# One clamp instead of two when float64 weights are converted, load targets in the result slots, and a compact RMS norm for batches 0 and 1

## The chip, the cores and the metric

The kernel runs on one core of one Trainium2 chip. The metric is the time of one execution in device microseconds. Three runs of the kernel before took 1404.11 to 1405.84 us, with a median of 1405.21 us.

## What is computed

Three stages follow each other. For 8 batches, 8 heads, 576 tokens and 64 features, linear attention (no softmax) with an RMS norm; then a feed-forward stage whose hidden layer is the maximum of three products; then one with a squared ReLU:

```python
kv = einsum('bhsd,bhse->bhde', k, v)
out = einsum('bhsd,bhde->bhse', q, kv)
out = out / sqrt(mean(out * out, axis=-1) + 1e-6) * g_norm      # per head
x = out as [8*576, 512]
h = maximum(maximum(x @ w1, x @ w2), x @ w3)                     # 512 -> 768
x = h @ w_out                                                    # 768 -> 512
r = maximum(x @ w_in, 0)                                         # 512 -> 2048
out = (s * (r * r) + b) @ w_out2                                 # 2048 -> 512
```

q, k, v and g_norm arrive as float32. The weight matrices arrive as float64 and are read by the kernel as 16-bit words, four to an element. Products are made in float32r as three matmuls of high and low parts (`mm3`: high times high, high weight times low activation, low weight times high activation), so each weight and each activation is split once into a high part (ScalarE, a rounding copy) and a low part (VectorE or GpSimd, a subtraction; both go through `hi_part` and `lo_part`, L263 and L266).

## The kernel before

Tokens are taken as 9 tiles of 512: tile j holds the first 512 tokens of batch j, the ninth the last 64 tokens of all batches. A tile is feature-major, 128 partitions (two heads, h and h + 4 of one **chunk** p, p = 0 to 3) by 512 tokens.

**Order of the work.** Nearly all work up to the last batch is written as jobs: `job(position, engine, cost, function, ..., r, w, a)` names what is read, written and allocated. `arrange` (L71) takes jobs in order of position as priorities: on each engine it starts the ready job with the lowest place in that order, as soon as the engine is free by the planner's own costs, and the list so made is issued as it stands. So each engine (PE, ACT, DVE, POOL) and the load queue SP runs its instructions in that fixed order, and waits where the real times differ from the planner's. A tag has a ring of buffers (`SIZE`; one where nothing is said), and a job that allocates waits for the last use of the buffer that it takes. Positions count in weight tiles; batch 0's start stands at Z = -12 and later, batch j's first layer at 22 j.

**Attention.** `load_kv`, `load_rem` and `load_q` (L301 to L333) bring k, v and q per chunk; `kv_mm` (L318) makes k^T v; `q_turn` (L337, VectorE) transposes q; `o_mm` (L350, L356) multiplies two chunks (half u) into one PSUM tile with tag "o" of two banks (one buffer), in quarters of 64x64; `o_out` (L360, ScalarE) copies it to SBUF.

**Norm, per chunk** (`plan_norm`): square (L366, ScalarE); `ms_mm` (L385, TensorE) multiplies by a 128x128 matrix that holds 1/64 in two blocks, so that each of the 64 rows of a head holds its mean square: for batches 0 and 1 (`bb < PLAIN`) one float32 matmul, which shows in the trace as two records; `rsqrt` (L394, L396, L399, ScalarE: logarithm, exponential, square) and `newton` (L404, L406, L409, VectorE): one Newton step and the multiplication by g. Then `x_hi` and `x_lo` split the chunk. Batches 2 to 7 split the square, too (`sq_hi`, `sq_lo`).

**First layer.** 18 weight tiles w0 to w17 (128 columns of w1, w2 or w3 in turn, all 512 rows: 128 partitions x 512 elements), each used by 12 matmuls (L155 to L157) per token tile (`plan_g1`); every three of them end in a copy and two maxima (L439, L441) and a split of h. For batch 0, w0 to w3 are used chunk by chunk as chunks are finished; from w4 on a tile takes all four chunks. **Second layer:** 6 tiles o0 to o5 (`plan_g2`).

**Conversion of a float64 tile** (`plan_conv`, 24 tiles before and beside batch 0, 32 later ones p0 to p31 that are stored again as float32): `conv_load` (L213, SP) brings 512 KB, moved by one 16-bit word; `conv_c` (L221 ScalarE or, for every third w and o tile and all p tiles, L223 VectorE) clears the sign of the upper 16 bits into a tile of its own; `conv_t` (L237, L239, ScalarE) are two ReLUs that clamp the exponent from above and from below; `conv_r` (L228, VectorE) scales and clamps the mantissa; `conv_s` (L232, VectorE) sets the sign; `conv_sum` (L243, VectorE) joins both; `conv_hi` and `conv_lo` split the result into the pair slot w0 to w17 or o0 to o5. The 512 KB land in one of three staging tiles: `craw`, and two of the slots of o0 to o5, which are not yet used.

```python
def conv_t(key, n):
    t = st["tr", key][:, 0]
    if n == 0:
        act(out=t.bitcast(F32), in_=st.pop(("gc", key)), func=AF.Relu, scale=-1.0, bias=lim[:, 0:1])
    else:
        act(out=t, in_=t.bitcast(F32), func=AF.Relu, scale=-float(2 ** 19), bias=lim[:, 1:2])
...
    sets = [("craw", "ctr", "cgc"), tuple(WOS[3:]), tuple(WOS[:3])]
```

After the batches the second feed-forward stage runs in products of quarters with fewer multiplications (L761, L839); the change does not touch it.

## Time and profile before

| | |
|---|---|
| median of three runs | 1405.21 us |
| the profiled execution | 1407.22 us |
| its span, first to last instruction | 1405.40 us |
| mean granted TensorE clock | 0.999 of 2.4 GHz |
| TensorE busy | 1370.8 us (98%), 6960 matmuls |
| VectorE busy | 908.3 us (65%) |
| ScalarE busy | 760.0 us (54%) |
| GpSimd busy | 244.4 us (17%) |
| DMA | 202.5 MB, 144 GB/s over the span |

The span is one execution on the hardware profiler. Shares are means over stages with different limits, so the stretches of the span are to be read one by one. A matmul record is longer than the matmul's share of the engine, since matmuls overlap: in an unbroken stream the starts tell the pace. "Clock" is the clock that TensorE was granted, as a part of 2.4 GHz.

### The profile page before, as it was taken

The numbers are of one execution on the slowest core, as the hardware profiler recorded it, in microseconds if no ns is written. First come the engines' busy times: TensorE is split into PE (matmuls) and PEld (weight loads), VectorE is DVE, ScalarE is ACT, GpSimd is POOL, SyncE is SP. The second block draws the span as 40 slices with busy tenths as digits, with TensorE's granted clock in tenths as the row PEclk, the third lists the DMA queues.
The fourth block names the chain that finished last, engine by engine and source line by source line (L and its number), as shares of the span: only waits on it lengthen the run. The fifth ranks groups of instructions, "written<-read, shape, count | busy, mean of one in ns | idle before, by whom it ended". The sixth has DMA issues, their size and how long they took to land. (4 is left out here: it accounts for less than half of the span.)

```text
span 1405.4 us, 19416 instructions
## 1 busy us (share of the span) xinstructions
PE 1370.8 (98%) x6960; PEld 1118.7 (80%) x6960; DVE 908.3 (65%) x1460; ACT 760.0 (54%) x1345; POOL 244.4 (17%) x173
## 2 busy tenths in 40 slices
PE   5999999999999999999999999999999999999997
PEld 3768888888888888888788789877888888888887
DVE  5995736363646452444747757467877978888884
ACT  6884435253434342333556456556775656566565
POOL 0001313132323122211000000000003314141412
PEclk9999999999999999999999999999999999999999
DMA  9876263625453310030354635544684454544441
GB/s 244 236 212 161 68 175 92 168 76 156 98 155 79 105 46 30 1 120 0 124 209 172 236 144 195 173 163 160 207 301 151 147 198 150 180 148 148 155 143 38
DMA packets 229169, 202.52 MB, mean 144 GB/s; under 512 B 126032, under 2 KB 183376, under 8 KB 226896
## 3 DMA queue, kind: packets, MB, share of 16 engines
q1 hardware_dynamic: 228912, 201.02, 46.1%
q8 instruction: 54, 0.88, 0.3%
q14 instruction: 43, 0.35, 0.1%
q10 hardware_dynamic: 160, 0.26, 0.0%
HBM read 126.79 MB, written 74.45 MB: 143 GB/s over the span
## 5 line engine op out<-in xcount | busy, mean ns | idle before, releaser
L155 PE MATMUL g<-xh,w_w 128*128 128x512 f32 x648 | 257.6, 398 | 0.7 <-ACT h L439 0.6
L156 PE MATMUL g<-xl,w_w 128*128 128x512 f32 x648 | 253.1, 391 | 1.5 <-DVE xl L266 1.5
L157 PE MATMUL g<-xh,w_w 128*128 128x512 f32 x648 | 253.3, 391 | 0.1
L151 ACT ACTIVATE zx<-z 128x512 fp32r<-128x512 f32 (+1 forms) x280 | 161.3, 587 | 123.1 <-PE zs_a L839 35.2
L761 PE MATMUL ps_a<-x_q,w_q 128*128 128x512 f32 (+1 forms) x960 | 210.5, 371 | 5.2 <-DVE cs L669 4.1
L839 PE MATMUL zs_a<-zx,w_q 128*128 128x512 f32 (+1 forms) x960 | 203.8, 369 | 0.5 <-POOL zx L152 0.3
L761 PEld LDWEIGHTS ps_a<-x_q,w_q 128*128 128x128 f32 x960 | 167.1, 188 | 40.0 <-DVE cs L669 7.2
L152 DVE TENSOR_TENSOR zx<-z,zx 128x512 fp32r<-128x512 f32 (+1 forms) x234 | 172.5, 755 | 34.8 <-ACT zx L151 34.5
L839 PEld LDWEIGHTS zs_a<-zx,w_q 128*128 128x128 f32 x960 | 167.9, 188 | 32.0 <-POOL zx L152 0.7
L152 POOL TENSOR_TENSOR zx<-z,zx 128x512 fp32r<-128x512 f32 (+1 forms) x46 | 64.3, 1398 | 594.1 <-DMA gd<-cs 382.6
L441 DVE TENSOR_TENSOR h<-g,h 128x512 f32<-128x512 f32 x108 | 74.6, 691 | 136.0 <-PE g L157 130.5
L155 PEld LDWEIGHTS g<-xh,w_w 128*128 128x128 f32 x648 | 121.8, 188 | 29.1 <-ACT xh L263 1.5
L156 PEld LDWEIGHTS g<-xl,w_w 128*128 128x128 f32 x648 | 122.0, 188 | 28.3 <-DVE xl L266 2.8
L157 PEld LDWEIGHTS g<-xh,w_w 128*128 128x128 f32 x648 | 121.8, 188 | 27.1 <-DVE w_w L266 0.7
L266 POOL TENSOR_TENSOR h<-h,h 128x512 fp32r<-128x512 f32 x40 | 60.1, 1504 | 458.4 <-ACT h L263 458.4
L761 PE MATMUL ps_b<-x_q,w_q 128*128 128x512 f32 (+1 forms) x480 | 106.4, 369 | 1.6 <-ACT cs L772 1.1
L839 PE MATMUL zs_b<-zx,w_q 128*128 128x512 f32 (+1 forms) x480 | 103.9, 371 | 2.0 <-DVE zx L152 2.0
L263 ACT ACTIVATE h<-h 128x512 fp32r<-128x512 f32 x54 | 34.0, 630 | 126.1 <-DVE h L441 125.5
L839 PEld LDWEIGHTS zs_b<-zx,w_q 128*128 128x128 f32 x480 | 83.9, 188 | 19.0 <-DVE zx L152 3.3
L761 PEld LDWEIGHTS ps_b<-x_q,w_q 128*128 128x128 f32 x480 | 83.9, 188 | 18.1 <-ACT cs L772 1.8
L155 PE MATMUL g<-h,w_o 128*128 128x512 f32 x216 | 84.6, 391 | 0.0
L157 PE MATMUL g<-h,w_o 128*128 128x512 f32 x216 | 84.0, 389 | 0.0
(149 smaller groups left out, 2016.7 us busy)
## 6 DMA issues: line engine op xcount, KB each, us to landing
z<-gd SPq DMA_DIRECT2D x64, 512.0 KB
gd<-cs SPq DMA_DIRECT2D x96, 256.0 KB
z<-gd SPq DMA_DIRECT2D x48, 256.0 KB
x1d<-x SPq DMA_DIRECT2D x36, 256.0 KB
k<-in_k_dram SPq DMA_DIRECT2D x32, 256.0 KB
...
```

Of the source, the lines that this page charges most:

```text
L151: act(out=hi, in_=src, func=AF.Copy)
L152: eng.tensor_tensor(out=lo, in0=src, in1=hi.bitcast(F32), op=ALU.subtract)
L155: nc.tensor.matmul(ps, lhsT=w[:, 0, sl], rhs=xh, start=first, stop=False)
L156: nc.tensor.matmul(ps, lhsT=w[:, 0, sl], rhs=xl, start=False, stop=False)
L157: nc.tensor.matmul(ps, lhsT=w[:, 1, sl], rhs=xh, start=False, stop=last)
L263: act(out=out, in_=src, func=AF.Copy)
L266: eng.tensor_tensor(out=out, in0=src, in1=hi.bitcast(F32), op=ALU.subtract)
L441: nc.vector.tensor_tensor(out=st["h", m], in0=ps, in1=st["h", m], op=ALU.max)
L761: nc.tensor.matmul(ps, lhsT=w[:, a, c], rhs=x[:, b_], start=new and k == 0 and e == 0, stop=k == HK - 1 and e == 2, skip_group_check=True)
L839: nc.tensor.matmul(ps, lhsT=w[:, a, c], rhs=x[:, b_, :n], start=new and k_ == 0 and e == 0, stop=k_ == 3 and e == 2, skip_group_check=True)
```

## The change

Conversion: the absolute value is written into the fourth 16-bit word of each element of the raw tile itself (`mag16`), on ScalarE for all w and o tiles and on VectorE for the p tiles; a single ReLU with a scale of 2^19 and a bias of -896 x 2^23 gives the exponent; for odd w and o tiles (`QACT`) the mantissa is made on ScalarE as its complement, and the join becomes an exclusive or and an or in one operation. Every w and o tile is loaded into the slot that its own result will take; the intermediate tile `tr` of the w tiles rotates over `craw`, `ctr` and the slots of o5 and o4. Positions of the first loads and conversions move (w0 to w3: loads from -10.65, -9.65, ... to -8.65, -8.35, ...; conversions one later), and those of batch 0's first matmuls by 0.5.

Norm of batches 0 and 1: the four squares have four buffers (`SQ`); `msc_mm` multiplies a square by a 128x32 matrix whose first two columns hold 1/64 for one head each, into rows 32p to 32p+31 of one PSUM tile; `rsqrt_c` makes logarithm, exponential, square and two Newton operations once for two chunks (batch 0, 64 partitions) or four (batch 1, 128 partitions); `bc_mm` multiplies 32 rows by `spread`, which holds ones where a head's row is to go to its 64 output rows, for two chunks into one PSUM tile with tag "o"; `normed` (VectorE) multiplies o by g and by that. `spread` is made of an identity (`make_identity`, two GpSimd operations) by eight small VectorE operations with the memsets of `means`.

```diff
-    nc.vector.memset(lim[:, 0:1], float(1151 * 16))
-    nc.vector.memset(lim[:, 1:2], float(255 * 2 ** 23))
+    nc.vector.memset(lim[:, 0:1], -float(896 * 2 ** 23))
+    nc.vector.memset(lim[:, 1:2], float(2 ** 19 - 1))
...
+    means = at_.tile([P, 32], F32, name="means")
+    nc.vector.memset(means, 0.0)
+    for h in range(2):
+        nc.vector.memset(means[h * D:(h + 1) * D, h:h + 1], 1.0 / D)
+    ident = at_.tile([P, P], F32, name="ident")
+    make_identity(nc, ident)
+    pick = at_.tile([P, 16], F32, name="pick")[:, :2]
+    spread = at_.tile([P, 2, D], F32, name="spread")
+    nc.vector.tensor_tensor(out=pick, in0=ident[:, 0:2], in1=ident[:, 32:34], op=ALU.add)
+    for p in range(2, NP):
+        nc.vector.tensor_tensor(out=pick, in0=pick, in1=ident[:, 32 * p:32 * p + 2], op=ALU.add)
+    for h in range(2):
+        nc.vector.tensor_copy(out=spread[:, h], in_=pick[:, h:h + 1].to_broadcast([P, D]))
...
-    def conv_c(key, gc, eng):
-        st["gc", key] = gc()
+    def mag16(key):
+        return st["raw", key].rearrange("p (n f) -> p n f", f=4)[:, :, 3]
+    def conv_c(key, eng):
...
-            act(out=st["gc", key].bitcast(BF16), in_=top16(key).bitcast(BF16), func=AF.Abs)
+            act(out=mag16(key).bitcast(BF16), in_=top16(key).bitcast(BF16), func=AF.Abs)
...
-            ts(out=st["gc", key], in0=top16(key), scalar1=0x7FFF, scalar2=None, op0=ALU.bitwise_and)
-    def conv_r(key, tr):
-        t = st["tr", key] = tr()
+            ts(out=mag16(key), in0=top16(key), scalar1=0x7FFF, scalar2=None, op0=ALU.bitwise_and)
+    def conv_r(key, eng):
+        t = st["tr", key]
...
+        if eng == "ACT":
+            act(out=t[:, 1], in_=mid, func=AF.Relu, scale=-(2.0 ** -13), bias=lim[:, 1:2])
+            return
...
-    def conv_t(key, n):
-        t = st["tr", key][:, 0]
-        if n == 0:
-            act(out=t.bitcast(F32), in_=st.pop(("gc", key)), func=AF.Relu, scale=-1.0, bias=lim[:, 0:1])
+    def conv_t(key, tr):
+        t = st["tr", key] = tr()
+        act(out=t[:, 0], in_=mag16(key), func=AF.Relu, scale=float(2 ** 19), bias=lim[:, 0:1])
+    def conv_sum(key, eng):
+        t = st.pop(("tr", key))
+        if eng == "ACT":
+            stt(out=t[:, 0], in0=t[:, 1], scalar=2 ** 19 - 1, in1=t[:, 0], op0=ALU.bitwise_xor, op1=ALU.bitwise_or)
...
-            act(out=t, in_=t.bitcast(F32), func=AF.Relu, scale=-float(2 ** 19), bias=lim[:, 1:2])
-    def conv_sum(key):
-        t = st.pop(("tr", key))
-        nc.vector.tensor_tensor(out=t[:, 0], in0=t[:, 0], in1=t[:, 1], op=ALU.bitwise_or)
+            nc.vector.tensor_tensor(out=t[:, 0], in0=t[:, 0], in1=t[:, 1], op=ALU.bitwise_or)
...
     def o_sq(bb, p, src):
-        sq = st["sq", p] = at_.tile([P, N], F32, tag="sq", name=f"sq_{bb}_{p}")
+        sq = st["sq", p] = at_.tile([P, N], F32, tag=SQ[p] if bb < PLAIN else "sq", name=f"sq_{bb}_{p}")
...
-        if bb < PLAIN:
-            nc.tensor.matmul(ps, lhsT=onesf, rhs=st["sq", p], start=True, stop=True)
-            return
...
+    def msc_mm(bb, p0, n):
+        if p0 == 0:
+            st["msc"] = psa.tile([P, N], F32, tag="ms", name=f"msc_{bb}")
+        for p in range(p0, p0 + n):
+            nc.tensor.matmul(st["msc"][32 * p:32 * (p + 1)], lhsT=means, rhs=st["sq", p], start=True, stop=True,
+                             tile_position=(0, 32 * p))
+    def rsqrt_c(bb, p, n, i):
+        sl = slice(32 * p, 32 * (p + n))
+        if p == 0 and i == 0:
+            st["yc"] = at_.tile([P, N], F32, tag="y", name=f"yc_{bb}")
+            st["uc"] = at_.tile([P, N], F32, tag="u", name=f"uc_{bb}")
+        y, u, ms = (st[c][sl] for c in ("yc", "uc", "msc"))
+        if i == 0:
+            act(out=y, in_=ms, func=AF.Ln, bias=eps[sl])
+        elif i == 1:
+            act(out=y, in_=y, func=AF.Exp, scale=-0.5)
+        elif i == 2:
+            act(out=u, in_=y, func=AF.Square)
+        elif i == 3:
+            stt(out=u, in0=ms, scalar=EPS, in1=u, op0=ALU.add, op1=ALU.mult)
+        else:
+            stt(out=u, in0=u, scalar=-3.0, in1=y, op0=ALU.add, op1=ALU.mult)
+    def bc_mm(bb, p):
+        st["bc", p // 2] = psa.tile([P, 2, N], F32, tag="o", name=f"bc_{bb}_{p}")
+        for i in range(2):
+            sl = slice(32 * (p + i), 32 * (p + i + 1))
+            nc.tensor.matmul(st["bc", p // 2][:, i], lhsT=spread[sl].rearrange("p h d -> p (h d)"), rhs=st["uc"][sl],
+                             start=True, stop=True, tile_position=(32 * (p + i), 0))
+    def normed(bb, p):
+        o = st["o", bb, p]
+        stt(out=o, in0=o, scalar=g_sb, in1=st["bc", p // 2][:, p % 2], op0=ALU.mult, op1=ALU.mult)
...
-    def plan_conv(kk, src, pos, load, a, pr, gc, slot=None, store=None):
+    def plan_conv(kk, src, pos, load, a, pr, slot=None, store=None):
...
-        raw, tr, g = f"raw_{kk}", f"tr_{kk}", f"gc_{kk}"
-        ra, tra, gca = stage(a, pr, gc)
+        raw, tr = f"raw_{kk}", f"tr_{kk}"
+        ra, tra = stage(a, raw, [P, 4 * N], U16), stage(pr, tr, [P, 2, N], I32)
+        eng = "DVE" if kk[0] == "p" else "ACT"
+        reng = "ACT" if kk[0] != "p" and QACT(key) else "DVE"
         job(load, "SP", 2.23, conv_load, key, src, ra, w=[raw], a=[(a, raw)], lag=6.0 if kk[0] == "p" else 2.0)
-        eng = "ACT" if kk[0] != "p" and key[1] % 3 else "DVE"
-        job(pos, eng, 0.43 if eng == "DVE" else 0.63, conv_c, key, gca, eng, r=[raw], w=[g], a=[(gc, g)])
-        job(pos, "DVE", 0.43, conv_r, key, tra, r=[raw], w=[tr + ":r"], a=[(pr, tr)])
-        for i in range(2):
-            job(pos, "ACT", 0.71, conv_t, key, i, r=[g], w=[tr + ":t"])
+        job(pos, eng, 0.43 if eng == "DVE" else 0.63, conv_c, key, eng, r=[raw], w=[raw + ":c"])
+        job(pos, "ACT", 0.71, conv_t, key, tra, r=[raw + ":c"], w=[tr + ":t"], a=[(pr, tr)])
+        job(pos, reng, 0.43 if reng == "DVE" else 0.71, conv_r, key, reng, r=[raw], w=[tr + ":r"])
...
-        job(pos, "DVE", 0.69, conv_sum, key, r=[tr + ":r"], w=[tr + ":t"])
-        if slot:
+        job(pos, "DVE", 0.69, conv_sum, key, reng, r=[tr + ":r"], w=[tr + ":t"])
+        if store is None:
...
+    def plan_compact(bb, p, t, u, x, eng, o, sq):
+        ms, y, uu = (f"{c}c{bb}" for c in ("ms", "y", "u"))
+        n = WIDE[bb]
+        if p % n == n - 1:
+            p0 = p - n + 1
+            job(t + 3.3 * u, "PE", 1.0, msc_mm, bb, p0, n, r=[f"sq{bb}.{k}" for k in range(p0, p + 1)],
+                w=[f"{ms}:{k}" for k in range(p0, p + 1)], a=[] if p0 else [("ms", ms)])
+            for i in range(5):
+                job(t + (4 + 0.3 * i) * u, "DVE" if i > 2 else "ACT", 0.7 if i > 2 else 0.65, rsqrt_c, bb, p0, n, i,
+                    r=[[f"{ms}:{k}" for k in range(p0, p + 1)], [f"{y}:{p0}"], [f"{y}:{p0}"],
+                       [f"{ms}:{k}" for k in range(p0, p + 1)], [f"{y}:{p0}"]][i],
+                    w=[[f"{y}:{p0}"], [f"{y}:{p0}"], [f"{uu}:{p0}"], [f"{uu}:{p0}"], [f"{uu}:{p0}"]][i],
+                    a=[("y", y), ("u", uu)] if p0 == i == 0 else [])
+            for k in range(p0, p + 1):
+                b = f"bc{bb}.{k // 2}"
+                if k % 2 == 0:
+                    job(t + 5.5 * u + 0.01 * k, "PE", 1.0, bc_mm, bb, k, r=[f"{uu}:{p0}"], w=[f"{b}:{k}", f"{b}:{k + 1}"],
+                        a=[("ops", b)])
+                job(t + 6.6 * u + 0.01 * k, "DVE", 0.7, normed, bb, k, r=[f"{b}:{k}", "g_sb", f"o{bb}.{k // 2}:{k % 2}"],
+                    w=[f"o{bb}.{k // 2}:{k % 2}"])
+        job(x, "ACT", 0.63, x_hi, bb, p, r=o, w=[f"xh{bb}:{p}"], a=[("xh", f"xh{bb}"), ("xl", f"xl{bb}")] if p == 0 else [])
+        job(x + 0.01, "DVE", 0.69, x_lo, bb, p, nc.vector, r=[*o, f"xh{bb}:{p}"], w=[f"xl{bb}:{p}"])
     def plan_norm(bb, p, t, u, x, eng):
...
-        job(t, "ACT", 0.59, square, r=r, w=[sq], a=[("sq", sq)])
...
+        job(t, "ACT", 0.59, square, r=r, w=[sq], a=[(SQ[p] if bb < PLAIN else "sq", sq)])
+        if bb < PLAIN:
+            return plan_compact(bb, p, t, u, x, eng, o, sq)
...
+    SQ = ["sq", "sqh", "sql", "sqx"]
+    QACT = lambda key: key[1] % 2
+    CP, LP, LS = 4, 3.35, 0.3
+    WIDE = {0: 2, 1: 4}
...
-        plan_norm(0, p, c, 0.1, c + 0.8, "DVE")
+        plan_norm(0, p, c, 0.1, Z + p // 2 * 2 + 3.1 + 0.01 * p, "DVE")
...
-            plan_g1(0, g, Z + 7 + p + 0.01 * g, [p])
+            plan_g1(0, g, Z + 7.5 + p + 0.01 * g, [p])
...
-    sets = [("craw", "ctr", "cgc"), tuple(WOS[3:]), tuple(WOS[:3])]
+    sets = ["craw", "ctr", "o5", "o4"]
...
-        plan_conv(f"w{n}", w1_src(n), 0.85 * n - 3 if n > 3 else Z + 3 + n, 0.85 * n - 5 if n > 3 else Z + 1.35 + n, *sets[n % 3], slot=W1S[n])
-    sets = [sets[0], (HS[M1 - 1], HS[M1 - 2], "st")]
+        plan_conv(f"w{n}", w1_src(n), 0.85 * n - 3 if n > 3 else Z + CP + n, 0.85 * n - 5 if n > 3 else Z + LP + LS * n, W1S[n], sets[n % 4], slot=W1S[n])
...
-                  *sets[m % 2 if m < M1 - 1 else 0], slot=WOS[m])
+                  WOS[m], sets[m % 2], slot=WOS[m])
...
-                    plan_norm(bb, p, c, d, max(t + G1 + 0.2 + 0.5 * p, c + 7 * d), "POOL" if p < 3 and j else "DVE")
+                    plan_norm(bb, p, c, d, max(t + G1 + 0.2 + 0.5 * p, c + 7 * d) if j else 20 + 0.1 * p, "POOL" if p < 3 and j else "DVE")
...
         pos = SL + 6 + 4.5 * n
-        plan_conv(f"p{n}", p2_src(n), pos + 0.6, pos - 2.5, *("craw", "ctr", "cgc"), store=pos + 3.2)
+        plan_conv(f"p{n}", p2_src(n), pos + 0.6, pos - 2.5, "craw", "ctr", store=pos + 3.2)
...
```

## Rows read from the trace of the kernel before

**Rows 1.** Stretches: us; busy PE, PEld, DVE, ACT, POOL (count); clock, DMA share, GB/s

```profile
0.00:20.00 20.00, 9.71 (x87) 5.61 (x88) 6.53 (x18) 7.90 (x15) 1.19 (x6) 1.00 0.83 199
20.00:46.30 26.30, 21.46 (x162) 12.97 (x160) 25.29 (x46) 23.18 (x41) 0.00 (x0) 1.00 1.00 261
46.30:74.00 27.70, 27.53 (x126) 20.85 (x126) 26.96 (x50) 24.10 (x43) 0.00 (x0) 1.00 0.85 241
74.00:86.00 12.00, 8.98 (x70) 5.38 (x70) 12.00 (x22) 11.93 (x22) 0.00 (x0) 0.86 1.01 263
...
117.10:1380.00 1262.90, 1253.52 (x6211) 1031.98 (x6210) 800.28 (x1256) 659.25 (x1163) 238.25 (x161) 1.00 0.44 139
```

**Rows 2.** Waits to 110 us (SPq) and 150 us: total us, times, longest

```profile
SPq L213 <- DVE tr_o L232: 12.6, 5, 5.0
...
ACT c_o L221 <- DMA raw_o<-in_moe_w_dram: 3.6, 3, 2.8
PE ops L350 <- DVE qt L337: 3.6, 2, 1.8
```

**Rows 3.** Lines to 117.1 us, conversion: busy us, mean ns, idle before

```profile
L232 DVE SCALAR_TENSOR_TENSOR tr_o<-raw_o,tr_o 128x512 uint16<-128x512 uint16 x12 | 9.0, 751 | 0.0
...
L239 ACT ACTIVATE tr_o<-tr_o,lim 128x512 int32<-128x512 f32 x12 | 8.6, 716 | 0.1
...
L221 ACT ACTIVATE c_o<-raw_o 128x512 bf16<-128x512 bf16 x12 | 8.0, 665 | 3.6 <-DMA raw_o<-in_moe_w_dram 3.6
...
L228 DVE TENSOR_SCALAR tr_o<-raw_o 128x512 int32<-128x512 uint32 x12 | 5.1, 421 | 0.4 <-DMA raw_o<-in_moe_w_dram 0.4
```

**Rows 4.** Lines to 117.1 us, norm

```profile
L385 PE MATMUL ms<-sq,onesf 128*128 128x512 f32 x16 | 8.7, 625 | 4.2 <-ACT sq L366 3.3 <-DVE u L404 0.8
...
L409 DVE SCALAR_TENSOR_TENSOR o<-o,g_sb,u 128x512 f32<-128x512 f32 x8 | 6.0, 747 | 0.0
...
L404 DVE SCALAR_TENSOR_TENSOR u<-ms,u 128x512 f32<-128x512 f32 x8 | 5.4, 677 | 0.2 <-ACT u L399 0.2
L394 ACT ACTIVATE y<-ms,eps 128x512 f32<-128x512 f32 x8 | 5.4, 674 | 0.4 <-PE ms L385 0.3
...
L396 ACT ACTIVATE y<-y 128x512 f32<-128x512 f32 x8 | 5.0, 622 | 0.0
```

**Rows 5.** Timeline, TensorE: start us, us, instruction

```profile
54.76 1.09 PE L350 MATMUL ops<-qt,kvc 64*64 64x512 f32 x8
...
112.99 0.39 PE L156 MATMUL g<-h,w_o 128*128 128x512 f32 x1
113.22 0.39 PE L157 MATMUL g<-h,w_o 128*128 128x512 f32 x1
...
114.60 0.39 PE L156 MATMUL g<-h,w_o 128*128 128x512 f32 x1
```

**Rows 6.** Timeline, marks of the start, all engines

```profile
9.09 0.50 SPq L213 DMA_DIRECT2D raw_craw<-in_moe_w_dram  x1
...
13.88 0.98 SPq L213 DMA_DIRECT2D raw_o<-in_moe_w_dram  x1
...
22.94 0.49 PE L155 MATMUL g<-xh,w_w 128*128 128x512 f32 x1 [0.16 <-ACT xh L263]
...
26.24 1.03 ACT L360 ACTIVATE o<-ops 128x1024 f32<-128x1024 f32 x1 [0.38 <-PE ops L350]
...
41.48 0.70 DVE L266 TENSOR_TENSOR xl<-o,xh 128x512 fp32r<-128x512 f32 x1
42.08 0.70 DVE L243 TENSOR_TENSOR tr_o<-tr_o 128x512 int32<-128x512 int32 x1
...
46.38 0.50 PE L155 MATMUL g<-xh,w_w 128*128 128x512 f32 x1 [0.58 <-ACT h L439]
...
117.12 0.39 PE L155 MATMUL g<-xh,w_w 128*128 128x512 f32 x1
```

**Rows 7.** The tile of the identity at the kernel's end, ns min/median/max

```profile
masks.py:199 POOL TENSOR_SCALAR_AFFINE_SELECT unit<-unit x1: 363/363/363, 1328.0 to 1328.0; 128x128 f32<-128x128 f32 x1
```

More of the change, by code (lines that the diff above doesn't have):

```diff
@@ L232, in conv_s, with stage @@
         stt(out=r16, in0=top16(key), scalar=0x8000, in1=r16, op0=ALU.bitwise_and, op1=ALU.bitwise_or)
[L234 to L243 removed]
+    def conv_t(key, tr):
[5 more added lines that the diff above has]
+            stt(out=t[:, 0], in0=t[:, 1], scalar=2 ** 19 - 1, in1=t[:, 0], op0=ALU.bitwise_xor, op1=ALU.bitwise_or)
+        else:
+            nc.vector.tensor_tensor(out=t[:, 0], in0=t[:, 0], in1=t[:, 1], op=ALU.bitwise_or)
         st["f32", key] = t[:, 0].bitcast(F32)
[L246 to L254 removed]
+    def stage(tag, name, shape, dtype):
+        return lambda: (at_ if tag[0] == "c" else base).tile(shape, dtype, tag=tag, name=name)
     W16 = [w.bitcast(U16) for w in (w1, w2, w3, wo, wi, w2o)]
@@ L528, in square @@
             o_sq(bb, p, src())
[L530 to L535 removed]
+        job(t, "ACT", 0.59, square, r=r, w=[sq], a=[(SQ[p] if bb < PLAIN else "sq", sq)])
+        if bb < PLAIN:
+            return plan_compact(bb, p, t, u, x, eng, o, sq)
+        job(t + u, "DVE", 0.42, sq_hi, bb, p, r=[sq], w=["h" + sq], a=[("sqh", "h" + sq)])
+        job(t + 1.2 * u, "POOL", 1.3, sq_lo, bb, p, r=[sq, "h" + sq], w=["l" + sq], a=[("sql", "l" + sq)])
+        job(t + 3.3 * u, "PE", 0.46, ms_mm, bb, p, w=[ms], a=[("ms", ms)], r=["h" + sq, "l" + sq])
         for n in range(3):
```

12 lines of the change are left out of this document (removed).

## The prediction

> **What bounds the kernel now.** I read the stretches first. From 117.1 to 1380 us TensorE is busy 1253.52 of 1262.90 us while VectorE is busy 800 and ScalarE 659 [rows 1]: nothing that takes work from those two can shorten this part. So the change has to earn its time before 117.1 us, where the first batch's attention, the conversion of 24 weight tiles from float64, and batch 1's attention run together. There TensorE is idle 10.3 us before 20 us (waiting for q, k and v), 4.8 us to 46.3, 0.2 to 74 and 3.0 us from 74 to 86; in that last stretch the mean granted clock also reads 0.86, which costs 0.14 x 12 = 1.7 us [rows 1]. That is all there is to gain, and part of the first 10.3 us stays.
>
> Who makes TensorE wait? VectorE is busy 25.29 of 26.30 us, then 26.96 of 27.70, then 12.00 of 12.00; ScalarE 23.18, 24.10, 11.93; the DMA share is 1.00, 0.85 and 1.01 [rows 1]. The waits say which of them comes first: the load queue waited 12.6 us for VectorE's sign step (L232) to free the staging tiles in o0 and o3, and TensorE 3.6 us for q to be transposed there [rows 2]. So VectorE is the bound between 20 and 86 us, ScalarE is next, and the DMA is busy but is also held back by VectorE.
>
> **The change part by part, and its sum.**
>
> **Conversion.** The old tile costs ScalarE two clamps of 0.72 us (L239, and L237 before it) and, for 16 of 24, an absolute value of 0.67 us (L221); VectorE 0.42 us for the mantissa (L228) and, for 8 of 24, as much for the absolute value (L223, the same kind of operation) [rows 3]. The new one drops one clamp, puts all 24 absolute values on ScalarE, and for the 12 odd tiles the mantissa too. VectorE: 8 + 12 operations less, 20 x 0.42 = 8.4 us. ScalarE: 24 clamps less, 8 absolute values and 12 mantissas more: -24 x 0.72 + 8 x 0.67 + 12 x 0.72 = -3.3 us. No row shows an absolute value written with a stride, or a clamp that reads with one: the nearest, L221, reads with that stride and takes 0.67 us where the unstrided L396 takes 0.62 [rows 3, 4], so 0 to 0.05 us for each of some 60 operations, at most 3 us on ScalarE, and below nothing there is no reason for; I take 0, as ScalarE has the room. The 32 late tiles lose a clamp as well, under a TensorE that is busy 99%: nothing.
>
> **Norm.** A chunk now costs three ScalarE operations of 0.62 to 0.67 us (L394, L396) after its square, and three on VectorE (L404 and its like L406 at 0.68, L409 at 0.75) [rows 4]. Batch 0 does the five middle ones twice instead of four times, batch 1 once: VectorE loses 4 + 6 = 10 x 0.68 = 6.8 us, ScalarE 6 + 9 = 15 x 0.64 = 9.6 us. The final multiply stays, its operand now in PSUM; L404 reads PSUM at 0.68 [rows 4], so no dearer.
>
> Together VectorE loses 15.2 us and ScalarE 12.9. These durations overlap by some 0.08 us (a split of 0.70 us at 41.48 is followed by the next at 42.08 [rows 6]), so 13 and 11 us of their time.
>
> **TensorE.** Four mean products of two matmul records at 0.625 [rows 4] become, in batch 0, two narrow groups and two broadcasts, in batch 1 one and two. Their shapes (32 columns or 32 rows of the array) are in no row. Nearest are the head products in quarters: eight records on four quarters take 1.09 us [rows 5], as long as two records of a mean product. So 1.1 us a group if the strips run side by side: batch 1 three for four, batch 0 four for four. If they ran one after another, batch 1 would pay 4 + 4 for 4, about 4 us more. I take 0: the one group saved pays for the change of shape. What a visitor of another shape costs shows where a k·v group of batch 2 stands among output matmuls: these start 0.23 us apart, the last before it at 113.22 and the second after it at 114.60 [rows 5], so it costs 1.38 - 0.46 = 0.9 us. The Trainium skill (TensorEngine Tiling (Array Packing), Key Properties) says that changing the tiling mode drains the array; the old mean products had the weights' own shape and changed nothing. [...]
>
> **Start.** All 18 w1 tiles land in their own result slots and wait for no staging. The loads of w0 and w1, issued on SP at 9.09 (0.50 us) and 13.88 (0.98 us) ahead of k, v and q of chunks 2 and 3 [rows 6], move behind q of chunk 3. Those chunks' loads, SP's issue time ahead, come 1.5 us sooner and without 1 MB in front of them. Those of chunk 3 were multiplied in time for their copy at 26.24 [rows 6]; I put that copy at 24.2, 2 us sooner: the bounds are SP's 1.5 us and, with 1 MB at 261 GB/s [rows 1], 5.5; near the lower, as SP issues the q loads no faster. The identity adds two operations on GpSimd, the longer 0.36 us [rows 7], ahead of the two clears that the loads of k's and v's remainders wait for: at most 0.7 us on SP with q of chunk 0 behind it, less what the loads of k and v are already issuing; I take 0.2. The eight small VectorE operations of the set-up run while it waits for q (6.53 us busy of the first 20 [rows 1]); if one were to wait for the identity, it costs what GpSimd is late, under 1 us, before any q has landed.
>
> **The added wait.** The broadcast takes the PSUM tile "o" (one buffer), which the products of chunks 2 and 3 hold. So no chunk of batch 0 is finished before these are copied and squared: 24.2, copy 1.03 and two squares on ScalarE (0.62 as L396) [rows 4, 6], 26.4; broadcast 27.5; multiply 0.75, high part 0.62 (a plain ScalarE operation like L396): the first weight matmul at about 29, not 22.94 [rows 6]. Behind the broadcast on TensorE's queue stand the means of chunks 2 and 3 (28.6); then 3 x 0.64 and 2 x 0.68, a broadcast, multiplies and splits: the last chunk ready at 35.5, where it was 41.48 + 0.70 [rows 6]. VectorE from 23 on has a transpose and two small copies (1.3 us), six norm operations (4.4), four splits (2.8) and the conversions of w0 to w3 (sign 0.75, sum and low part 0.70 each, and 0.42 for the even ones [rows 3, 6]: 9.4), 17.9 us by durations, some 15 by starts: free at 38 to 41. The 48 matmuls of w0 to w3 need 48 x 0.23 = 11 us, the last 12 of them (2.7 us) after w3: they end between 40 and 43.4. I take 41, as the chunks set it more than w3 does. The matmuls of w4 started at 46.38 [rows 6]. Gain 5.4 us, bounds 3 to 6.4 if the order holds.
>
> **From w4 to batch 1.** The old stretch, 46.38 to 117.12 [rows 6], is 70.7 us, of which 0.2 + 3.0 idle and 1.7 of half clock: 4.9 to win. VectorE then has, by starts of about 0.6 us, 20 conversions of 2.0 us, 18 maxima and splits of h and 9.5 us of batch 1, 61 us for about 66, so those stalls can go. What is late next: w4 converted only 2 us after w3, and w8, whose load stands behind batch 1's k, v and q. Some 11.8 MB come before its end; the old trace moved 199 x 20 + 261 x 26.3 = 10.8 MB by 46.3 us [rows 1], so w8 lands near 51, is converted by 54.5, and is wanted at 41 + 4 tiles x 12 x 0.228 + 4 k·v groups x 0.92 = 55.6. I charge 5 us of new stalls, bounds 1 and 8.
>
> Sum: 5.4 + 4.9 - 5 = 5.3 us. The profiled execution took 1407.22 us around a span of 1405.40, 2.0 us above the median of the runs, 1405.21: it becomes 1402, and the median 1400.0.
>
> **The rivals.**
> *The DMA was the bound* (no change). For it: a share of 1.00 from 20 to 46.3 [rows 1]; the same bytes must land. Against: SP's waits for VectorE [rows 2]. Then only the 2 us at the start and what the stalls give are left: the w tiles land as before, gain 0 to 2.8, 1404.
> *ScalarE's queue stands still* (slower). Every absolute value is now on ScalarE, in order, ahead of squares and logarithms of the norm. When a weight tile lands later than the order assumed, the norm behind it waits; before, three such waits made 3.6 us, the longest 2.8 [rows 2], with a third of the tiles on VectorE. If each of the four tiles of the start holds ScalarE 2.5 us, w4 starts at 51, not 41, 4.6 us later than it did: 1405.2 + 4.6 - 4.9 + 5 = 1409.9. It decides once these waits exceed the 5.3 us of the sum. Against it: ScalarE has 11 us less to do, and the load queue waits for nothing.
> *Late start, half clock* (within 0.2%). TensorE has little from 24 to 29; in 74 to 86, with 3.0 us idle, the mean granted clock fell to 0.86 [rows 1]. Twice that price, 3.4 us, leaves a gain of 2: 1403. Against it: the stretch before 20 us was idle 10.3 of 20 and shows 1.00 [rows 1].
> *The strips don't run side by side*: 4 us in batch 1, hidden in batch 0, leave 1.3: 1404.
>
> **How the numbers follow.** A measurement tells 0.2% (2.8 us) from no change. Forecast: 0.60. DMA bound 0.14, half clock 0.07, serial strips 0.05, ScalarE's waits 0.14. The forecast's own range: best 6.4 + 4.9 - 1 + 1 (a broadcast less dear) = 11 us, 1394; worst 3 + 4.9 - 8 = -0.1, 1405. Of the forecast 0.02 lies within 0.2%; of the three milder rivals (0.26) 0.06 gain more than 2.8 us and 0.02 lose more. So faster 0.58 + 0.06 = 0.64, same 0.02 + 0.18 = 0.20, slower 0.14 + 0.02 = 0.16. For 8 in 10 the range runs from 1394.5 to 1408, leaving out the worst half of ScalarE's case.
>
> **What would show it.** Right: 24 fewer ACT clamps before 117 us; VectorE under 90% between 41 and 100; the first weight matmul near 29, w4's near 41, batch 1's first weight matmul near 112; SP's waits for the sign step gone. Wrong: w4's start at 46 or later; a broadcast of 2 us; ScalarE waiting for a w load with the norm behind it; TensorE idle over 8 us between w4 and batch 1.

## The result: 0.52% slower, and the profile after

The change takes 1412.28 us (median of 5 runs, 1410.03 to 1415.99) where the kernel before takes 1405.21: a ratio of 1.0052, with a 95% interval of 1.0033 to 1.0070. The forecast was 1400.0 in a range of 1394.5 to 1408.0. Both the sign and the range were wrong.

The profiled execution of the change took 1410.79 us around a span of 1409.0. The stretches of [rows 1] up to 117.1 us, with the same columns (us; busy PE, PEld, DVE, ACT, POOL with counts; granted clock, DMA share, GB/s):

```profile
0.00:20.00 20.00, 10.88 (x100) 5.79 (x102) 4.34 (x21) 5.60 (x10) 1.63 (x8) 1.00 0.85 176
20.00:46.30 26.30, 17.05 (x105) 9.05 (x100) 17.98 (x30) 22.41 (x32) 0.00 (x0) 0.81 1.06 278
46.30:74.00 27.70, 25.63 (x151) 18.76 (x149) 23.76 (x42) 24.29 (x34) 0.00 (x0) 1.00 1.16 313
74.00:86.00 12.00, 12.00 (x64) 9.20 (x64) 9.44 (x16) 11.94 (x17) 0.00 (x0) 1.00 1.28 165
86.00:117.10 31.10, 30.28 (x179) 21.14 (x178) 27.13 (x47) 28.55 (x41) 0.00 (x0) 1.00 0.34 110
```

Three things are to be seen. **VectorE is relieved as forecast**: 82.65 us of work before 117.1 us (the sum of its first five numbers), against 96.83 before, 14.2 us less where 15.2 were counted. **ScalarE is not**: 92.79 us against 88.40, 4.4 us more where 12.9 less were counted. **TensorE is idle 9.25 us from 20 to 46.3 us**, 4.8 before, and its mean granted clock there is 0.81. The row of the kernel before for 86 to 117.1 us, which the two sums need, and three shorter windows of the change, which show where its clock fell:

```profile
86.00:117.10 31.10, 31.10 (x166) 24.64 (x165) 26.05 (x48) 21.29 (x38) 0.00 (x0) 1.00 0.55 158
```

```profile
24.00:28.00 4.00, 1.09 (x4) 0.51 (x4) 1.30 (x4) 4.00 (x6) 0.00 (x0) 0.64 1.09 349
28.00:32.00 4.00, 2.84 (x8) 0.19 (x4) 2.97 (x5) 3.59 (x6) 0.00 (x0) 0.50 1.18 263
32.00:36.00 4.00, 3.48 (x26) 2.40 (x26) 2.94 (x5) 3.90 (x6) 0.00 (x0) 0.58 1.10 348
```

The groups by line up to 125 us (as [rows 3, 4]: busy us, mean ns of one | idle before) say what ScalarE does with the time:

```profile
L237 ACT ACTIVATE raw_w<-raw_w 128x512 bf16<-128x512 bf16 x18 | 24.0, 1364 | 0.0
...
L237 ACT ACTIVATE raw_o<-raw_o 128x512 bf16<-128x512 bf16 x6 | 7.9, 1366 | 0.0
```

The absolute value (L237) took 0.665 us as L221 [rows 3]; written into the raw tile it takes 1.364. Twenty-four of them are 24 x 0.70 = 16.8 us more than the sum had, and -12.9 + 16.8 is within 0.5 of the 4.4 measured.

Now TensorE's timeline from the last products of batch 0 on (start us, us, instruction, in brackets the idle time before it and what ended it):

```profile
22.59 1.08 PE L362 MATMUL ops<-qt,kvc 64*64 64x512 f32 x4 [2.14 <-DVE qt L349]
...
26.91 2.08 PE L428 MATMUL bc<-uc,spread 32*128 32x512 f32 x4 [3.13 <-ACT sq L378]
28.92 1.92 PE L404 MATMUL msc<-sq,means 128*32 128x512 f32 x4
32.52 0.80 PE L155 MATMUL g<-xh,w_w 128*128 128x512 f32 x1 [1.68 <-ACT w_w L275]
33.11 0.63 PE L156 MATMUL g<-xl,w_w 128*128 128x512 f32 x1
33.54 0.63 PE L157 MATMUL g<-xh,w_w 128*128 128x512 f32 x1
...
99.07 1.07 PE L404 MATMUL msc<-sq,means 128*32 128x512 f32 x8
...
107.00 1.13 PE L428 MATMUL bc<-uc,spread 32*128 32x512 f32 x4
...
122.17 0.39 PE L155 MATMUL g<-xh,w_w 128*128 128x512 f32 x1
```

A broadcast of two chunks takes 1.13 us at 107 us and 2.08 at 26.91; two matmuls of the first layer start 0.43 us apart at 33 us, where a stream goes at 0.23 [rows 5]. In the windows from 24 to 36 us the granted clock is 0.64, 0.50 and 0.58: TensorE is at 1.2 GHz for most of them, after waiting. Its first weight matmul comes at 32.52 us, not 22.94 [rows 6], and what it waits for last is the high part of w0 (L275); w4's first (the 49th of the layer) at 51.80, not 46.38; batch 1's first at 122.17, not 117.12. So the start loses 5.4 us and the stretch from w4 to batch 1 wins 0.4.

ScalarE's timeline of the same moments shows what the broadcast's 3.13 us wait is made of: copy, square, an absolute value of 1.33 us that puts the second square 1.1 us later (25.10 to 26.17), and that square. It also shows when the high parts of x and of w0 are made.

```profile
23.70 1.02 ACT L372 ACTIVATE o<-ops 128x1024 f32<-128x1024 f32 x1 [2.99 <-PE ops L362]
24.62 0.59 ACT L378 ACTIVATE sq<-ops 128x512 f32<-128x512 f32 x1
25.10 1.33 ACT L237 ACTIVATE raw_w<-raw_w 128x512 bf16<-128x512 bf16 x1
26.17 0.69 ACT L378 ACTIVATE sq<-ops 128x512 f32<-128x512 f32 x1
...
29.81 1.29 ACT L275 ACTIVATE xh<-o 128x512 fp32r<-128x512 f32 x2 [0.30 <-DVE o L433]
...
31.84 0.63 ACT L275 ACTIVATE w_w<-tr_w 128x512 fp32r<-128x512 f32 x1
```

### The profile page after: what moved, and what is told of

Read it like the earlier page. It is cut to its first block, busy times and chain, and to the rows that moved or that the text cites. A ratio compares the mean times of both kernels' runs of the same rounds, so it can differ in the third digit from the quotient of the medians.

```text
span 1409.0 us, 19416 instructions
## 1 busy us (share of the span) xinstructions
PE 1372.2 (97%) x6976; PEld 1117.3 (79%) x6976; DVE 912.8 (65%) x1438; ACT 748.0 (53%) x1294; POOL 237.5 (17%) x175
## 5 line engine op out<-in xcount | busy, mean ns | idle before, releaser
L278 POOL TENSOR_TENSOR h<-h,h 128x512 fp32r<-128x512 f32 x40 | 54.7, 1367 | 464.3 <-ACT h L275 464.3
L275 ACT ACTIVATE h<-h 128x512 fp32r<-128x512 f32 x54 | 34.0, 630 | 133.4 <-DVE h L485 133.0
```

Source lines behind the costliest of these rows:

```text
L275: act(out=out, in_=src, func=AF.Copy)
L278: eng.tensor_tensor(out=out, in0=src, in1=hi.bitcast(F32), op=ALU.subtract)
```

## The experiments

Four suspects can be taken out one at a time: the **strided write** of the absolute value; the **compact norm of batch 0** with its broadcast behind chunk 3; that of **batch 1**; and the **later loads and conversions** of w0 to w3. Ratios are to the kernel before on the same chip, with 95% intervals.

### What makes the absolute value slow

`act_forms` is the kernel before with extra operations at its start, three of each kind, on a tile of constants; its time, with that work added, says nothing.

```diff
+        act(out=pb[:, :N].bitcast(BF16), in_=lane(pa, 2).bitcast(BF16), func=AF.Abs)       # L266
+        act(out=lane(pb, 3).bitcast(BF16), in_=pa[:, :N].bitcast(BF16), func=AF.Abs)       # L267
+        act(out=lane(pa, 3).bitcast(BF16), in_=lane(pa, 2).bitcast(BF16), func=AF.Abs)     # L268
...
```

> The kernel before with measuring operations at its start, on scratch tiles, that change nothing of the result: the absolute value of 512 16-bit words per partition on ScalarE in seven forms (read and written contiguous or one word in four, in place or into another tile, one word in two, contiguous in place, 32-bit results at 8-byte pitch), and the bitwise form on VectorE in three. Theory A1 (16-bit words written at 8-byte pitch are slow whatever is read): the forms that write one word in four take 1.3 to 1.4 us, also into another tile and from a contiguous source, the others 0.6 to 0.7. Theory A2 (it is the writing into the tile that is read): only the forms in place are slow, the contiguous one in place too. VectorE: 0.42 us contiguous, 0.72 strided. The time says nothing here; the operations are timed one by one.

The groups by line of these operations (busy us, mean ns of one | idle before). `lane(t, i)` takes every fourth 16-bit word, a pitch of 8 bytes:

```profile
L269 ACT ACTIVATE pb<-pa 128x512 bf16<-128x512 bf16 x3 | 4.2, 1390 | 0.0
L267 ACT ACTIVATE pb<-pa 128x512 bf16<-128x512 bf16 x3 | 4.0, 1346 | 0.1
L268 ACT ACTIVATE pa<-pa 128x512 bf16<-128x512 bf16 x3 | 4.0, 1338 | 0.1
L270 ACT ACTIVATE pb<-pa 128x512 bf16<-128x512 bf16 x3 | 2.3, 777 | 0.0
...
L274 DVE TENSOR_SCALAR pb<-pa 128x512 uint16<-128x512 uint16 x3 | 2.2, 737 | 0.1
L272 ACT ACTIVATE pb<-pa 128x512 f32<-128x512 bf16 x3 | 2.1, 684 | 0.1
L266 ACT ACTIVATE pb<-pa 128x512 bf16<-128x512 bf16 x3 | 2.0, 664 | 2.7 <-DVE pb L274 1.3 <-DVE pb L260 1.3
L271 ACT ACTIVATE pa<-pa 128x512 bf16<-128x512 bf16 x3 | 1.9, 632 | 0.1
...
L273 DVE TENSOR_SCALAR pb<-pa 128x512 uint16<-128x512 uint16 x3 | 1.3, 427 | 0.0
```

Reading at that pitch costs next to nothing (664 against 632 ns). Writing 16-bit results at it doubles the time, whether the tile is the same (1338) or another (1346), and whether the read is strided (1390) or not. At a pitch of 4 bytes it is 777, and 32-bit results at 8 bytes take 684. So it is the scattered 16-bit write, not working in place. VectorE pays, too: 427 to 737.

`own_tile` is the change with only that write undone:

```diff
+        st["gc", key] = at_.tile([P, N // 2], U32, tag="cgc", bufs=2, ...).bitcast(U16)
-            act(out=mag16(key).bitcast(BF16), in_=top16(key).bitcast(BF16), func=AF.Abs)
+            act(out=st["gc", key].bitcast(BF16), in_=top16(key).bitcast(BF16), func=AF.Abs)
```

> The changed kernel with one thing undone: the absolute value goes into a contiguous tile of its own again (two buffers) instead of the fourth word of the raw tile. In the trace of the changed kernel that operation takes 1364 ns (24 times to 117 us) against 665 ns before, 24 x 0.70 = 16.8 us of ScalarE, which is busy 97% from 34 to 110 us. Theory A (the strided write made ScalarE the bound): the operation is back at 0.67 us, ScalarE falls by about 17 us before 117 us, and the time falls by 7 to 11 us, to 1401 to 1405. Theory B (the price is the late start and the half clock from 25 to 35 us, from the broadcast behind the products of chunks 2 and 3): the operation is at 0.67, but the time stays within 3 us of the changed kernel's 1412.

1405.56 us, ratio 1.0012 (1.0003 to 1.0021): 6.7 us under the change's time, 5.6 by the ratios, short of theory A's 7 to 11. (From 34 to 110 us ScalarE was busy 71.84 of 76 us in the change, 95% and not 97%.) The absolute value is back at its old price, by the groups of this kernel's lines:

```profile
L238 ACT ACTIVATE c_w<-raw_w 128x512 bf16<-128x512 bf16 x18 | 11.7, 662 | 0.0
```

Batch 1 begins at 117.02 us and not at 122.17: of the 16.8 us of ScalarE's time, 5.1 had reached the path by then. So the write is the larger part of the loss; but what is left is still not faster than before, and its clock from 20 to 46.3 us is 0.81 as in the change.

### Conversion or norm

`conv_only` is the change with the norm of before (`plan_norm`, `ms_mm`), `norm_only` the kernel before with the compact norm of both batches.

```diff
 # conv_only
-        if bb < PLAIN:
-            return plan_compact(bb, p, t, u, x, eng, o, sq)
 # norm_only: conv_c to conv_sum, stage, sets and the load and conversion positions of before;
 # the first layer's positions are the change's
```

> The changed conversion, loads and slots with the norm of before (a mean product per chunk, no broadcast). Theory A: the strided write still costs ScalarE 16.8 us and the old norm 9.6 us more, so it is slower than the changed kernel: 1413 to 1420. Theory B: the ring wait of the broadcast is gone, the first weight matmul comes sooner: 1400 to 1407.

1412.0 us, 1.006 (1.0047 to 1.0073): as slow as the whole change, between the ranges of the two theories. Its first weight matmul comes at 32.43 us, so the late start does not need a broadcast.

> The kernel before with the compact norm alone (conversion, staging tiles and load order as before). Theory A: VectorE and ScalarE have 7 and 10 us less to do, nothing is dearer: 1400 to 1405. Theory B: the first weight matmul waits for the products of chunks 2 and 3 and the clock falls: 1408 to 1414.

1407.28 us, 1.0029 (1.0018 to 1.0040). That is between the two ranges, nearer to theory B's. So the compact norm (with the change's positions for the first matmuls), with nothing of the slow write in it, loses, though it takes work from both engines. Windows of 4 us of norm_only, from 24 us on (columns as above):

```profile
24.00:28.00 4.00, 1.98 (x8) 0.82 (x8) 2.40 (x7) 1.82 (x5) 0.00 (x0) 0.62 1.13 342
28.00:32.00 4.00, 3.46 (x8) 0.69 (x8) 2.81 (x7) 3.43 (x6) 0.00 (x0) 0.50 1.13 266
32.00:36.00 4.00, 4.00 (x29) 3.07 (x28) 3.61 (x8) 3.85 (x7) 0.00 (x0) 0.60 1.10 348
```

VectorE and ScalarE have time to spare; TensorE is idle for 2 of the first 4 us, its granted clock reads 0.62, 0.50 and 0.60, and its work there is done mostly at half pace. Its first weight matmul comes at 33.66 us.

### The wait for the PSUM tile, and the clock

The first theory on norm_only was the wait that the change adds: the broadcast takes the tile "o", so nothing of batch 0 is finished before chunk 3 is copied. `norm_ring` (norm_only) and `own_ring` (own_tile) give the broadcast of chunks 0 and 1 two banks of the ring "g" instead; `own_ring_early` also has the positions of before for the first loads and conversions.

```diff
+            st["bc", p + i] = o[:, i] if bb or p else psg.tile([P, N], F32, tag="g", ...)
 # own_ring_early, too
-    CP, LP, LS = 4, 3.35, 0.3
+    CP, LP, LS = 3, 1.35, 1
-            plan_g1(0, g, Z + 7.5 + p + 0.01 * g, [p])
+            plan_g1(0, g, Z + 7 + p + 0.01 * g, [p])
```

> The kernel before with the compact norm alone, as norm_only (1407.3 us, 1.0029 of before), but the broadcast of chunks 0 and 1 of batch 0 goes into two banks of the ring g instead of the tile o that the products of chunks 2 and 3 hold, so that it needn't wait for them and the first weight matmuls stand in TensorE's queue before the means of chunks 2 and 3. Theory B1 (the wait for the tile o is what the norm costs: TensorE has nothing to do from 24 to 28 us and its clock falls to half from 25 to 35): the first weight matmul starts at 23 to 26 us instead of after 30, the granted clock stays at 1.00, and the time falls by 3 to 7 us, to 1400 to 1404. Theory B2 (the norm costs something else, for instance its matmuls of another shape): the time stays within 2 us of 1407.

1411.66 us, 1.0033 (1.0019 to 1.0048): not told apart from norm_only. The first broadcast did come earlier, at 23.85 us, but the products of chunk 3 now stood behind it, at 28.19, and the first weight matmul came at 30.31 where 23 to 26 was expected.

> own_tile with the broadcast of chunks 0 and 1 in two banks of the ring g, as in norm_ring. w0 is still loaded behind q of chunk 3, so the first weight matmul can't come before w0 is converted (31.8 us in own_tile, where it waited for w0's high part on ScalarE). Theory B1: the broadcast comes 2 to 3 us sooner, ScalarE splits x before it converts w0; the gain is 0 to 2 us, 1403.5 to 1405.5. If the ring alone was the price of the late start, 1401 to 1402.5.

1408.03 us, 1.0012 (1.0002 to 1.0023): as own_tile. Taking the wait for the PSUM tile away wins nothing here. That it costs nothing is not shown: in neither kernel did the first weight matmul come early, as another wait took its place (in own_ring it came at 33.88, behind w0's high part).

> own_ring with the loads of w0 to w3 and their conversions where the kernel before has them (w0 behind q of chunk 1, w1 behind q of chunk 2), and the first matmuls' position as before. If the late start comes from both the tile o and the load order: the first weight matmul starts at 24 to 26 us, the clock stays at 1.00 or nearly, and the time is 1397 to 1401, under both kernels. If the load order doesn't matter: as own_ring within 1 us.

1405.31 us, 0.9991 (0.9980 to 1.0003): the earlier loads are worth 0.2%, less than expected; the clock still read 0.63 and 0.51 from 24 to 32 us.

`own_warm` tests the clock: own_tile with three matmuls of no use on TensorE after the products of chunk 3, and three more after the second group of means.

```diff
+        for _ in range(3):
+            nc.tensor.matmul(ps, lhsT=onesf, rhs=st["sq", n], start=True, stop=True)
```

> own_tile (1405.6 us) with six float32 matmuls more on TensorE, whose result nobody reads: three behind the products of chunk 3 (about 23.6 to 26.2 us, where TensorE waited for the squares) and three behind the means of chunks 2 and 3. They change only whether TensorE is busy there. If the half clock itself (0.65, 0.50, 0.57 in the three stretches of 4 us from 24 to 36 in own_tile) costs time: the clock stays at 1.00, the broadcast's 2.08 us and the means fall to 1.1, and the time falls by 2 to 4 us, to 1401.5 to 1403.5. If the stretch is set by ScalarE and the loads whatever the clock: it stays within 1 us of 1405.6, or rises by the matmuls' own time.

1405.66 us, 0.9987 (0.9978 to 0.9996), 0.25% under the ratio of own_tile, and of own_ring, which ran on the same chip with 1408.03: work added makes it faster. Windows of own_tile, then of own_warm:

```profile
28.00:32.00 4.00, 2.31 (x7) 0.36 (x6) 3.40 (x6) 2.85 (x6) 0.00 (x0) 0.50 1.19 261
32.00:36.00 4.00, 3.80 (x26) 2.58 (x26) 3.15 (x5) 3.93 (x7) 0.00 (x0) 0.57 1.10 347
```

```profile
24.00:28.00 4.00, 4.00 (x6) 1.39 (x5) 1.29 (x4) 3.97 (x7) 0.00 (x0) 0.61 1.10 351
28.00:32.00 4.00, 4.00 (x13) 1.31 (x13) 2.68 (x5) 1.97 (x4) 0.00 (x0) 1.00 1.20 254
32.00:36.00 4.00, 3.46 (x29) 1.82 (x27) 2.94 (x5) 3.88 (x7) 0.00 (x0) 1.00 1.10 347
36.00:40.00 4.00, 2.80 (x6) 1.20 (x7) 3.59 (x7) 3.77 (x8) 0.00 (x0) 0.67 1.10 348
```

From 28 to 36 us the clock is full; but it was at half for most of the window before, and it falls again for a part of the 10 us after, where TensorE waits. So in this execution the half clock is moved more than cured: from 20 to 60 us it takes some 5 us of full clock here (means of 0.85 and 0.90 in the two stretches of 20 us) as in own_tile (0.74 and 1.00). Its mean clock, 0.996, is the lowest of own_warm's 12 runs, so the gain is read from the runs, and no trace shows where a usual one has it. Over all runs the mean granted clock has a median of 0.998 in own_warm, 0.9935 in own_tile and 0.997 to 0.998 in the runs of the kernel before. A difference of 0.0045 over 1403 us is 12.6 us more at 1.2 GHz, or 6.3 us of full clock, of which only the part with TensorE busy is lost work.

### Undoing the rest, one at a time

The last four all have own_tile's conversion. `own_conv_only` has the norm of before, `own_norm1` has it for batch 0 alone and the compact one for batch 1; each with the change's first loads and with those of before (`_early`, the diff above). The positions of a batch's splits go with its norm.

```diff
 # own_norm1, against own_tile
-        if bb < PLAIN:
+        if bb == 1:
             return plan_compact(bb, p, t, u, x, eng, o, sq)
```

> The changed conversion with the absolute value in a contiguous tile of its own, and the norm of before. If the two costs add (the strided write 6.7 us, by the pair after and own_tile; the compact norm 0.29%, by norm_only), taking 0.29% from own_tile's 1.0012 gives a ratio of 0.998 to before, with the clock at 1.00 until 70 us. If they do not add, and the conversion alone is what is late (conv_only at 1.006 less 0.0048 for the strided write), it is 1.001 to 1.002, and the clock falls to half in this one too.

1405.59 us, 0.9991 (0.9981 to 1.0001): nearer to "the costs add" than to 1.001. But the clock falls to half here as well (0.89, 0.50, 0.50 and 0.83 in the windows from 24 to 40 us), without a compact norm. TensorE's timeline of own_conv_only shows the wait in which it fell:

```profile
25.98 1.13 PE L398 MATMUL ms<-sq,onesf 128*128 128x512 f32 x2 [1.93 <-ACT sq L379]
31.25 0.80 PE L155 MATMUL g<-xh,w_w 128*128 128x512 f32 x1 [4.15 <-ACT w_w L276]
```

What TensorE waits for last, 4.15 us long, is the high part of w0, which the change loads and converts later.

> As own_conv_only, with the first loads and conversions at the positions that they had before. If the later loads of w0 to w3 cost the start (the step from own_ring to own_ring_early was 0.2%), this is 0.2% under own_conv_only: 0.996 if the costs add, 1.000 if they do not. If the earlier loads only helped there because the norm was compact, the two are the same within 0.1%.

1402.97 us, 0.9972 (0.9960 to 0.9983): 0.19% under own_conv_only, as expected for the loads; the level lies between the two that were expected.

> Conversion in a contiguous tile of its own, norm of batch 0 as before, compact norm for batch 1 alone. If the harm of the compact norm is in batch 0 (TensorE with little to do from 24 to 36 us, at half clock), it is gone here and batch 1's relief of ScalarE (9 operations of 0.64 us) and VectorE (6 of 0.68 us) stays: as own_conv_only or up to 0.2% better, 0.996 to 0.998, clock 1.00 to 70 us. If the harm is in batch 1's broadcasts on TensorE (1.13 us each, other shapes), it is no better than own_tile, 1.001.

1403.41 us, 0.9976 (0.9968 to 0.9985): in the range expected. But the clock, expected to stay at 1.00, reads 0.55 and 0.60 from 28 to 36 us, after a wait of 4.01 us for w0's high part.

> As own_norm1, with the first loads and conversions at the positions that they had before. The best of all by the theory that costs add: 0.995 to 0.997. If nothing but TensorE's idle time in the first 20 us is left to win, it is within 0.1% of own_norm1.

1400.58 us against 1406.52 for the kernel before beside it, 0.9953 (0.9940 to 0.9967): faster than both kernels. Its windows from 20 us on:

```profile
20.00:24.00 4.00, 2.99 (x31) 1.44 (x27) 3.69 (x7) 3.97 (x8) 0.00 (x0) 1.00 1.16 242
24.00:28.00 4.00, 3.15 (x14) 1.36 (x14) 4.00 (x8) 3.26 (x7) 0.00 (x0) 1.00 1.09 344
28.00:32.00 4.00, 3.29 (x24) 1.90 (x24) 2.79 (x6) 3.91 (x8) 0.00 (x0) 1.00 1.18 245
32.00:36.00 4.00, 3.08 (x24) 2.02 (x26) 3.57 (x6) 4.00 (x8) 0.00 (x0) 1.00 1.10 348
```

TensorE is never idle for more than 1.1 of 4 us, and the clock is full there and in every later window to 118 us.

All kernels but act_forms in one table. "First", "w4" and "batch 1" are the starts of the first matmul of the first layer, of its 49th, and of batch 1's first, in the profiled execution of each; "clock" is the median over all runs of the mean granted clock. Each execution's marks are one sample, so the ratios decide.

| kernel | write | first loads | norm, batch 0 / 1 | first | w4 | batch 1 | clock | ratio |
|---|---|---|---|---|---|---|---|---|
| before | own tile | early | old / old | 22.94 | 46.38 | 117.12 | 0.997, 0.998 | 1 |
| the change | strided | late | compact / compact | 32.52 | 51.80 | 122.17 | 0.994 | 1.0052 |
| conv_only | strided | late | old / old | 32.43 | 52.32 | 126.35 | 0.9935 | 1.0060 |
| norm_only | own tile (before's) | early | compact / compact | 33.66 | 49.62 | 118.65 | 0.994 | 1.0029 |
| norm_ring | own tile (before's) | early | compact, ring g / compact | 30.31 | 53.18 | 123.31 | 0.9925 | 1.0033 |
| own_tile | own tile | late | compact / compact | 31.83 | 50.26 | 117.02 | 0.9935 | 1.0012 |
| own_ring | own tile | late | compact, ring g / compact | 33.88 | 55.01 | 120.97 | 0.993 | 1.0012 |
| own_ring_early | own tile | early | compact, ring g / compact | 28.02 | 49.00 | 115.91 | 0.996 | 0.9991 |
| own_warm | own tile | late | compact / compact, more matmuls | 32.81 | 52.92 | 119.65 | 0.998 | 0.9987 |
| own_conv_only | own tile | late | old / old | 31.25 | 50.90 | 119.32 | 0.9955 | 0.9991 |
| own_conv_early | own tile | early | old / old | 24.51 | 47.87 | 115.50 | 0.998 | 0.9972 |
| own_norm1 | own tile | late | old / compact | 31.09 | 50.38 | 115.93 | 0.996 | 0.9976 |
| own_norm1_early | own tile | early | old / compact | 23.83 | 45.99 | 112.71 | 0.999 | 0.9953 |

The steps can be read off by pairs. From the best kernel up: later loads +0.23% (to own_norm1), batch 0's compact norm +0.36% (to own_tile), the strided write +0.40% (to the change). (Without the compact norms the write costs more, 0.69%: from own_conv_only to conv_only.) The steps down: the conversion with one clamp and its landing slots -0.28% (before to own_conv_early), batch 1's compact norm -0.15% and -0.19% (own_conv_only to own_norm1, and the same early). The step for the loads is the same within 0.04% at three places (own_ring, own_conv_only, own_norm1). Each ratio is known to 0.1 to 0.2% either way, the change's worst, a step between two to somewhat more: that of batch 1 rests on having come out twice.

The steps for the loads and for batch 1 are pairs on one chip. Batch 0's step is not: own_norm1 and own_tile ran on different chips. norm_only, which has both compact norms, speaks for it: if the two add, batch 0's is 0.29 + 0.15 to 0.19 = 0.44 to 0.48% there. Where own_tile loses it is not shown: w4 starts at 50.38 us in own_norm1 and at 50.26 in own_tile, batch 1 at 115.93 and 117.02. In both the first weight matmul waits for w0's high part (4.01 and 1.69 us), so with late loads the first matmul is set by w0 and not by the norm; the mean clock is 0.996 and 0.9935.

## Why the prediction was wrong, point by point

**The step that failed first** is this one: "No row shows an absolute value written with a stride ... the nearest, L221, reads with that stride and takes 0.67 us ... so 0 to 0.05 us for each". A row on a strided read was taken for a strided write. It measured 0.70 us, 24 times, 16.8 us on the engine that was to be relieved by 12.9, and costs 0.40% or 5.6 us of the kernel's time (own_tile to the change). The Trainium skill (ScalarE: Activation LUTs, What ACT_TABLE_LOAD costs) gives an ACTIVATE one element per cycle per lane for every function, fp32 and bf16 alike; with the fixed cost that it states, 512 elements are an estimated 0.61 us. That section says nothing of the layout of what is written. The rows agree for contiguous results (0.63), strided reads (0.66) and 32-bit results at 8 bytes (0.68), and not for 16-bit results at a pitch of 4 (0.78) or 8 bytes (1.34 to 1.39).

**"From w4 to batch 1 ... 4.9 to win", less "5 us of new stalls".** With the write at its old price the stalls do not come: 66.76 us in own_tile (50.26 to 117.02), where it was 70.74. That is 4.0 of the 4.9, so the charge of 5 was too much. In the change itself the slow ScalarE takes the gain away: 70.37.

**"Gain 5.4 us, bounds 3 to 6.4"** for the start was a loss of 5.4. The forecast put the copy at 24.2, the broadcast's end at 27.5 and the first matmul at 29 us; they came at 23.70, 28.99 and 32.52. So the chain was right up to the broadcast's start, forecast for 26.4. It left out two things. One is the clock: the broadcast took 2.08 us where 1.1 was planned, in the stretch that the prediction itself called one with little to do, and the 48 matmuls planned at 0.23 us began at 0.43. The other is w0: "I take 41, as the chunks set it more than w3 does" did not ask when w0 is ready. Its high part was made from 31.84 us on, when those of x were done (31.10); the first matmul waited 1.68 us for it, and 4.15 in own_conv_only. The loads of w0 and w1 that moved behind q were counted only for what they cleared for others, not for what they themselves came late for, and that is 0.2%. Batch 0's norm, whose saved operations the sum counted as a gain, costs 0.36% by the table.

**"Late start, half clock"** stood among the rivals at 0.07 and 3.4 us, with the idle first 20 us at full clock against it. It happened, in every kernel of the table whose first weight matmul came at 28 us or later, and for a shorter time in own_conv_early (0.72 and 0.85 from 24 to 32 us), where it came at 24.51. And the argument against it was a misreading. The column does read 1.00 before 20 us, but the starts in the trace of the kernel before show half pace there:

```profile
8.77 1.97 PE L350 MATMUL ops<-qt,kvc 64*64 64x512 f32 x4 [1.79 <-DVE qt L337]
10.50 0.31 PE L356 MATMUL kvor<-qt,kvc 64*64 64x64 f32 x1
...
18.38 1.08 PE L350 MATMUL ops<-qt,kvc 64*64 64x512 f32 x4 [1.20 <-ACT kvc L323]
19.29 0.22 PE L356 MATMUL kvor<-qt,kvc 64*64 64x64 f32 x1
```

The same four matmul records keep TensorE for 1.73 us from 8.77 and for 0.91 from 18.38. So the idle start was no counterexample, and the mean clocks given here leave that stretch out.

The price of the half clock from 20 us on lies between own_warm's 0.25%, for curing part of it, and the steps for batch 0's norm and the loads together, 0.59% or 8 us, in which TensorE's waits have their share. Among the runs of one kernel the time follows the mean clock: in the change, own_tile, own_ring and norm_ring by 0.8 to 1.2 us for each 0.001 (a line fitted to each kernel's runs). By that the 0.0055 between own_tile and own_norm1_early would be an estimated 4 to 6.5 of the 8 us. This is a correlation and no experiment, so how the loss divides between the waits and the clock is not settled: own_norm1_early, in which TensorE is kept fed, is rid of both.

**"ScalarE's queue stands still"** gave the right sign and mark (w4 at 51; it was 51.80), but by luck: ScalarE does not wait for a w tile's load anywhere to 118 us, and with the short operations of own_tile w4 still starts at 50.26. So 1.5 of the 5.4 us go with the longer operations, and the rest is there without them. That rival was priced at 1409.9.

**Right:** VectorE's relief (14.2 us of 15.2); the load queue's 12.6 us of waits for the sign step are gone (5.6 us for VectorE's low part of a w tile came in their place); the strips run side by side, four chunks' means in 1.07 us and two broadcasts in 1.13. For the change of shape the sum took nothing, as the one group saved was to pay for it. The timeline of own_tile, at 108 us:

```profile
108.43 0.39 PE L157 MATMUL g<-h,w_o 128*128 128x512 f32 x1
108.75 1.13 PE L429 MATMUL bc<-uc,spread 32*128 32x512 f32 x4
109.81 0.50 PE L155 MATMUL g<-h,w_o 128*128 128x512 f32 x1
110.14 0.40 PE L156 MATMUL g<-h,w_o 128*128 128x512 f32 x1
```

The starts before and after the broadcast are 0.32 and 0.33 us apart instead of 0.23: 0.2 us for this visit beside its own 1.06. The Trainium skill (TensorEngine Tiling (Array Packing), Key Properties) states that changing the tiling mode drains the array. These starts are in line with that; the cost is small, as taken. A gain of the size that was forecast, 5.3 us, exists: own_norm1_early has 0.47%, 6.6 us. That the sizes are near is in part luck, since the parts are others: to w4 it gains 0.4 us and not 5.4, and from w4 to batch 1 4.0 (66.72 us against 70.74) and not the -0.1 of 4.9 - 5. Three parts of the change that the sum had at nothing, or as gains, hid it.
